# Pieces of x, loads further ahead and later weight parts in a retention and two-MLP kernel

## The chip, the cores and the metric

The kernel runs on one core of a Trainium2 chip. The metric is the device time of one execution in microseconds (us); the time before is the median of three runs. A traced execution gives the profile.

## The reference, cut to what matters

A retention layer (a linear attention with a decay per head) over 4 sequences of 768 tokens, 8 heads of 64, and behind it two MLPs over the 3072 tokens, with 512 features and 2048 hidden units:

```python
for t in range(S):
    state = gamma * state + einsum('bhd,bhe->bhde', k[:, :, t], v[:, :, t])
    y[:, :, t] = scale * einsum('bhd,bhde->bhe', q[:, :, t], state)
x = y.transpose(0, 2, 1, 3).reshape(3072, 512)
h = x @ w_in;  x = (h * cos(h)) @ w_out                    # first MLP
h = x @ w_in2                                              # second MLP
g = where(h >= 1, h, where(h <= -1, 0, (h + 1) ** 2 / 4))
out = g @ w_out2
```

All inputs are float32. The kernel's products are made of high and low parts: a matrix is split into a rounded part and the rest, and three of the four products of parts are summed.

## The kernel before, in words

Tokens run in six blocks of 512 (b = 0 to 5); hidden units in 16 slices of 128, in two halves of eight (k = 0, 1). One step is one slice of one block: `first` multiplies x by a slice of w_in (12 matmuls of 512 columns into one PSUM bank, line 642), `act` makes h cos h of it, and `second` (12 matmuls, line 729) multiplies the result by a slice of w_out into four banks that gather over eight steps. `second` runs three steps behind `first`. There are 48 steps for k = 0 and 48 for k = 1. In the first 40, attention is done in between, chunk by chunk of 128 tokens, and `first` alternates between two banks (line 1457 on); in the other 56 it uses four. The kernel is written in the order of execution for each engine; nothing is rescheduled. The second MLP, from about 640 us on, is a fast matrix product of seven half-size products (class `Products`); only its first group is touched by the change.

In `act` ScalarE rounds h to whole turns (`rounded`, line 680), VectorE takes the fraction (line 685), ScalarE the sine (line 691); a step later VectorE multiplies (line 694), ScalarE makes the high part gh (line 698) and VectorE the low part gl (line 705), which is the last to read the bank of h. The results of a block are read out by `evacuate` (lines 740 to 747): four tiles of 512 columns, made by VectorE and ScalarE, and stored by SP. For k = 1 the stored result of k = 0 is added. The tiles come from a ring of five buffers named r, which `rounded` uses too.

Data that move meanwhile: x, made by attention or needed again for k = 1, is stored by ScalarE's queue (`store_parts`, high and low part, 1 MB each) and loaded by SP (`load_parts`); partial results by `load_part`. Attention's operands for a chunk (q and k as qk and kq, v, the keys kd, the state's increments vw) are loaded by SP, as many steps ahead as the table `lead` says. Weights come as 64-bit floats of 512 KB per slice (raw) and are converted by a conveyor (`Convert`, `Conveyor`): `load`, and some steps later `one` (VectorE), `two` (ScalarE, line 192), `three` (VectorE), `four` (GpSimd, line 209), `five`. For the second MLP, `five` calls `combine`: GpSimd makes four sums of quarters of two slices (line 246), `seven` and `eight` then split them and the quarters into high parts (ScalarE, line 139) and low parts (GpSimd, line 142), and SP stores these (`send_parts`). The numbers in the conveyor's table are the steps between the load and each of these. Ready weights are weights that were converted earlier and stored; they are only loaded.

The right sides of the fast product, differences of quarters of the first MLP's output, are made by `right_sides(0)` in 22 small items, one a step: GpSimd's subtractions (line 825) and again high and low parts.

Each engine works its instructions off in order, and SP and ScalarE also issue DMAs. A program waits for a DMA at one of eight counters that SP and ScalarE share in turn, and the issue of a DMA first waits until the DMA that used the same counter before has landed, which is the one eight places before it in the program's order.

Of the kernel before, what the change touches and what calls it, by code (L numbers as in the profile page):

```python
# [40 lines left out]
def tile_retention_mlp_mlp(  # L41
# [113 lines left out]

    class Convert:
# [4 lines left out]
        def __init__(self, m, j, a, keep, late=False, ready=False, store=False):  # L161
            self.m, self.j, self.a, self.keep, self.late, self.ready = m, j, a, keep, late, ready
            self.store = store or not late

        def load(self, stage):
            self.stage = stage
            if self.ready:
                self.f = self.stage.tile([P, TB], F32, tag="cf", name="cf", bufs=5)
                nc.sync.dma_start(out=self.f, in_=w32_d[self.m, self.j, self.a])
                return  # L170
            self.raw = self.stage.tile([P, TB, 2], I32, tag="raw", name="raw", bufs=3 - self.late)
            src = (w1, w2)[self.m][self.j][:, self.a * TB:(self.a + 1) * TB]
            nc.sync.dma_start(out=self.raw.rearrange("p n w -> p (n w)"), in_=src.bitcast(I32))

        def one(self):
            if self.ready:
                return
            ncs, ncf = ((3, 3), (1, 5))[self.late]
            self.s = self.stage.tile([P, TB], I32, tag="cs", name="cs", bufs=ncs)
            self.f = self.stage.tile([P, TB], F32, tag="cf", name="cf", bufs=ncf)  # L180
# [44 lines left out]
        def combine(self):  # L225
# [55 lines left out]
    class Conveyor:  # L281
# [40 lines left out]
    class Attention:  # L322
# [41 lines left out]
        def load_t(self, n):  # L364
# [4 lines left out]
            if n >= NEW:  # L369
# [6 lines left out]
                self.kq[n] = self.ring("kq", 3 * TB // 2, 2)  # L376
                nc.sync.dma_start(out=self.kq[n], in_=kq[n - NEW])
# [6 lines left out]
        def load_v(self, n):  # L384
# [14 lines left out]
            for r in range(2):  # L399
# [214 lines left out]

    def store_parts(b):
        for t, d in zip(xt[0, b], xT_d[b]):
            nc.scalar.dma_start(out=d, in_=t.bitcast(F32))

    def load_parts(b):

        x_tiles(1, b)
        for t, d in zip(xt[1, b], xT_d[b]):
            nc.sync.dma_start(out=t.bitcast(F32), in_=d)

    def load_part(b):

        for t, d in zip(xt[1, b], (yp_d[b], yq_d)[:1 + (b == 0)]):
            t = t.bitcast(F32)
            nc.sync.dma_start(out=t, in_=d)
            for e in range(NP):  # L630
# [119 lines left out]
    class Products:  # L750
# [76 lines left out]
        def make(self, c):  # L827
# [14 lines left out]
            def parts(q):  # L842
# [9 lines left out]
                lambda: self.sums(x, ("t2", "22", "t1"), ("t4", "21", "t2")),  # L852
            ] + [lambda q=q: parts(q) for q in TURN]
# [363 lines left out]
        def run(self, before):  # L1217
# [13 lines left out]
            for g in range(self.NG + 1):  # L1231
                if g == 0:
                    ends = iter([f for b in before for f in (b, lambda: None)])
# [11 lines left out]
                if g == 0:  # L1245
# [4 lines left out]
                    top.append(self.ps)  # L1250
                    self.pairs += [("wo", n) for n in range(NH + NP + 1, NF - 1)]
# [7 lines left out]
    def run():  # L1259
        i = 0  # L1260
        with ExitStack() as es:
# [155 lines left out]
            plan = {n: [[] for _ in range(6)] for n in range(NH * (NB - 1))}  # L1417
            for n in range(CB, NCH):
                c = n % CB
                if n < 3 * CB:  # L1420
                    i = 11 * (n // CB - 1) + c
                    lead = (3, 1, 0) if n < 2 * CB else (3, 3, 1)
                else:
                    i = NH * (n // CB - 1) + 2 * c
                    lead = (4, 2, 1)
                plan[i][3 if n >= 3 * CB else 4].append(n)
                plan[i + 1][5].append(n)
                for k in range(3):
                    if n >= CB + (CB, 1, 1)[k]:
# [3 lines left out]
            for i in range(NH * (NB - 1)):  # L1433
                load_t, load_v, decay, early, late, attend = plan[i]
# [3 lines left out]
                for n in load_t:  # L1438
                    att.load_t(n)
                for n in load_v:  # L1440
# [44 lines left out]
                if i in (6, 9):  # L1485
                    store_parts(i // 9)
# [9 lines left out]
        with ExitStack() as es:  # L1496
# [5 lines left out]
            while i < len(steps):  # L1502
# [34 lines left out]
            assert not todo and not ready and not any(conv.slots[-4:])  # L1537
# [94 lines left out]
```

## Time and profile before

| | before |
|---|---|
| runs | 1117.85, 1118.36, 1120.42 us |
| median | 1118.36 us |
| profiled execution | 1123.43 us, of which span 1121.6 us |
| TensorE, matmuls | 1079.9 us busy (96% of the span) |
| VectorE, GpSimd, ScalarE | 802.5, 613.8, 602.1 us busy |
| DMA | 279.9 MB, mean 250 GB/s |
| mean granted clock | 0.987 |

Busy matmuls overlap each other, so the share of TensorE says that it seldom stands, not that it is at its peak. The granted clock is 1 at 2.4 GHz and 0.5 at 1.2 GHz, the two levels in this trace. Where TensorE stands, the trace names the engine and line that released it.

### The profile page before, as it was taken

The page shows a single profiled execution, that of the slowest core. Times are in us where ns is not written, and L with a number is a line of the kernel's source. Part 1 is how long each engine was busy: PE and PEld are TensorE (multiplying, and loading weights), DVE is VectorE, ACT ScalarE, POOL GpSimd, SP SyncE. Part 2 cuts the span into 40 slices and gives each one's busy share as a digit, 9 for nine tenths or more (in the row PEclk, how much of TensorE's full clock was granted, in tenths as well). Part 3 has the DMA queues.
Part 4 walks back from the last instruction along what each step waited for, and adds up shares of the span by engine and source line. Part 5 has one row for each costly group of instructions (what it writes and reads, how often), then busy time and mean ns, then how long its engine had stood idle before and what let it go on. Part 6 is the DMA issues. An engine that isn't in the chain of part 4 may idle for free.

```text
span 1121.6 us, 17830 instructions
## 1 busy us (share of the span) xinstructions
PE 1079.9 (96%) x6286; PEld 873.4 (78%) x6286; DVE 802.5 (72%) x1101; ACT 602.1 (54%) x1078; POOL 613.8 (55%) x525
## 2 busy tenths in 40 slices
PE   7997999989999999999899999999999999999996
PEld 5676777868888888887688878787888788888884
DVE  5776867766766635677786377677888778977776
ACT  3453333323444644555555376676757677666663
POOL 3834202221225655789998057696648786464642
PEclk9999999989999999999999999999999999999999
DMA  9559488785749778878797666979779889576542
GB/s 326 176 197 318 119 236 283 223 290 179 251 137 329 254 257 288 287 290 303 240 342 250 241 219 217 316 237 361 254 221 317 305 293 387 172 243 207 182 150 85
DMA packets 126504, 279.94 MB, mean 250 GB/s; under 512 B 14032, under 2 KB 40272, under 8 KB 122448
## 3 DMA queue, kind: packets, MB, share of 16 engines
q1 hardware_dynamic: 119792, 257.31, 69.0%
q10 hardware_dynamic: 6624, 21.50, 4.9%
q8 instruction: 50, 0.82, 0.3%
q14 instruction: 38, 0.31, 0.1%
HBM read 195.39 MB, written 83.36 MB: 249 GB/s over the span
## 4 chain that ended last, share of the span: by engine, by line
PE 79%; DVE 6%; DMA 5%; POOL 5%; issue 3%; ACT 2%; SPq 1%; DVEq 0%; ACTq 0%; POOLq 0%
PE b L729 20%; PE b L642 20%; PE b L911 17%; PE y L927 17%; PE b L557 1%; PE b L464 1%; DMA qk<-in_qk 1%; POOL s L246 1%; DVE big L993 1%; DMA xb1t20h<-xhi 1%; POOL cf L209 1%; POOL cf L142 1%; DVE cf L185 1%; DMA xb2t20h<-xhi 1%; PE b L475 1%
## 5 line engine op out<-in xcount | busy, mean ns | idle before, releaser
L685 DVE SCALAR_TENSOR_TENSOR r<-b,r 128x512 f32<-128x512 f32 x96 | 66.1, 689 | 141.0 <-ACT r L680 140.4
L209 POOL TENSOR_TENSOR cf<-cf,cs 128x512 int32<-128x512 int32 x64 | 83.2, 1300 | 144.3 <-DVE cf L200 115.3
L680 ACT ACTIVATE r<-b 128x512 int32<-128x512 f32 x96 | 56.9, 593 | 193.3 <-PE b L642 157.3
L985 DVE TENSOR_TENSOR xh<-y,xh 128x1024 f32<-128x1024 f32 x88 | 107.1, 1221 | 27.9 <-PE y L927 26.8
L1063 POOL TENSOR_TENSOR ft<-r,f 128x512 f32<-128x512 f32 x24 | 31.1, 1296 | 139.9 <-PE y L927 93.0
L729 PE MATMUL b<-gh,wo 128*128 128x512 f32 x384 | 100.2, 396 | 5.2 <-DVE o L740 5.2
L927 PE MATMUL y<-wi,wo 128*128 128x512 f32 x360 | 92.7, 392 | 3.9 <-POOL wi L952 2.2
L642 PE MATMUL b<-xh,wi 128*128 128x512 f32 x384 | 94.9, 389 | 0.0
L729 PEld LDWEIGHTS b<-gh,wo 128*128 128x128 f32 x384 | 72.4, 191 | 22.5 <-ACT wih L139 4.6
L911 PE MATMUL b<-wih,wi 128*128 128x512 f32 x320 | 88.0, 393 | 0.4 <-DVE b L1055 0.4
L985 DVE TENSOR_TENSOR xl<-y,xl 128x1024 f32<-128x1024 f32 x64 | 77.9, 1217 | 13.8 <-PE y L927 13.8
L927 PE MATMUL y<-gh,wo 128*128 128x512 f32 x272 | 85.4, 396 | 2.3 <-DVE xh L985 2.3
L642 PE MATMUL b<-xh,wih 128*128 128x512 f32 x192 | 77.6, 407 | 7.7 <-DVE gl L705 6.1
L642 PEld LDWEIGHTS b<-xh,wi 128*128 128x128 f32 x384 | 72.1, 188 | 15.0
L927 PEld LDWEIGHTS y<-wi,wo 128*128 128x128 f32 x360 | 66.9, 188 | 20.8 <-POOL wi L952 3.7
L729 PE MATMUL b<-gh,woh 128*128 128x512 f32 x192 | 78.1, 412 | 0.5 <-ACT woh L139 0.5
L642 PE MATMUL b<-xh,wil 128*128 128x512 f32 x192 | 76.3, 400 | 0.0
L698 ACT ACTIVATE gh<-b 128x512 fp32r<-128x512 f32 x96 | 57.1, 595 | 35.0 <-DVE b L694 35.0
L729 PE MATMUL b<-gh,wol 128*128 128x512 f32 x192 | 74.5, 393 | 0.0
L952 POOL TENSOR_TENSOR gl<-ft,gh 128x512 fp32r<-128x512 f32 x56 | 71.7, 1298 | 1.3 <-ACT gh L139 1.3
L911 PEld LDWEIGHTS b<-wih,wi 128*128 128x128 f32 x320 | 60.3, 189 | 13.8 <-DVE b L1055 1.3
L691 ACT ACTIVATE r<-r 128x512 f32<-128x512 f32 x96 | 60.5, 631 | 15.2 <-DVE r L685 15.1
(164 smaller groups left out, 2752.9 us busy)
## 6 DMA issues: line engine op xcount, KB each, us to landing
wi<-wp SPq DMA_DIRECT2D x66, 512.0 KB, 4.9
wo<-wp SPq DMA_DIRECT2D x66, 512.0 KB, 5.1
raw<-in_w SPq DMA_DIRECT2D x64, 512.0 KB, 5.5
wp<-whi SPq DMA_DIRECT2D x48, 256.0 KB, 2.5
wp<-s SPq DMA_DIRECT2D x32, 256.0 KB, 2.2
w<-cf ACTq DMA_DIRECT2D x26, 256.0 KB, 3.8
xTh<-xh ACTq DMA_DIRECT2D x6, 1024.0 KB, 6.7
xTl<-xl ACTq DMA_DIRECT2D x6, 1024.0 KB, 8.8
```

Of the source, the lines that this page charges most:

```text
L209: nc.gpsimd.tensor_tensor(out=f, in0=f, in1=self.s, op=ALU.add)
L642: nc.tensor.matmul(out=h, lhsT=w[:, c * P:(c + 1) * P], rhs=x[:, c, :], start=(i == 0), stop=(i == len(terms) - 1),)
L680: nc.scalar.activation(out=self.r.bitcast(I32), in_=self.h, func=AF.Identity, scale=INV_2PI, bias=0.25)
L685: nc.vector.scalar_tensor_tensor(out=self.r, in0=self.h, scalar=INV_2PI, in1=self.r.bitcast(I32), op0=ALU.mult, op1=ALU.subtract,)
L691: nc.scalar.activation(out=self.r, in_=self.r, func=AF.Sin, scale=TWO_PI, bias=HALF_PI)
L698: nc.scalar.activation(out=self.gh, in_=self.h, func=AF.Copy)
L729: nc.tensor.matmul(out=acc[k, b][e], lhsT=w[:, s], rhs=g, start=(begin and i == 0), stop=(last and i == 2),)
L911: nc.tensor.matmul(out=to, lhsT=w[:, c * P:(c + 1) * P], rhs=x, start=begin and n == 0, stop=n == len(terms) - 1, skip_group_check=not begin,)
L927: nc.tensor.matmul(out=to[:, e, :], lhsT=w[:, e * P:(e + 1) * P], rhs=a, start=begin and m == 0, stop=m == 2, skip_group_check=not begin,)
L952: eng.tensor_tensor(out=lo, in0=self.f.pop((g, q)), in1=hi.bitcast(F32), op=ALU.subtract)
L985: nc.vector.tensor_tensor(out=a, in0=y, in1=a, op=ALU.add)
L1063: nc.gpsimd.tensor_tensor(out=o, in0=x, in1=z, op=ALU.subtract)
```

## The change

x moves in pieces: `store_parts` and `load_parts` only list pieces of one of four feature groups (256 KB); `send_x` issues two of them on ScalarE behind each step, `fetch_x` three on SP. Blocks 0 and 1 are listed after steps 3 and 6, where their stores stood at steps 6 and 9. Partial results come in two halves. Attention's loads get a table with four columns (q, k and state together; kq; v and keys; decay). In the stage of the second MLP's weights the conveyor has one step more before `one` and two more before `seven` and `eight`, one more raw buffer, and keeps its parts in weight buffers that are free by then (`spare_tile`) in place of two-buffer rings. `right_sides(0)` starts at the first step of the fifth block for k = 1 (before: the fifth step of the third), one item a step in that block and two in the last. The last second products stand one place later in the first group of the fast product, and its accumulators' tiles are named once before use.

```diff
+    spare = (
+        {
+            "f": [f"il{n}" for n in range(NH)] + [f"ol{n}" for n in range(6)],
+            "s": [f"ih{n}" for n in range(NH)],
+            "whi": [f"oh{n}" for n in range(NH)] + ["ol6", "ol7"],
+        },
+        {
+            "f": ("il1", "il3", "il5", "il7", "ol1", "ol3"),
+            "s": ("ih3", "ih5", "ih7", "ih1"),
+            "whi": ("oh1", "oh3", "oh5", "oh6", "oh7", "ol5", "ol6", "ol7"),
+        },
+    )
+    spare = [{nm: itertools.cycle(tags) for nm, tags in d.items()} for d in spare]
+
+    def spare_tile(nm, few, dt=F32):
+        return wpool[0].tile([P, TB], dt, tag="w" + next(spare[few][nm]), name=nm)
...
+            self.few = (j // 2 * 4 + a * 2 + j % 2) > 18
...
-            self.raw = self.stage.tile([P, TB, 2], I32, tag="raw", name="raw", bufs=3 - self.late)
+            self.raw = self.stage.tile([P, TB, 2], I32, tag="raw", name="raw", bufs=3 + self.late)
...
-                t = wpool[0].tile([P, TB], F32, tag=f"wo{'hl'[n]}6", name=f"s{n}")
+                t = spare_tile("s", self.few)
...
-            if n in (1, 2):
-                hi = self.stage.tile([P, TB], F32R, tag="whi", name="whi", bufs=2)
-            else:
-                hi = wpool[0].tile([P, TB], F32R, tag=f"wo{'hl'[n // 3]}7", name="whi")
+            hi = spare_tile("whi", self.few, F32R)
...
-                order = (("five", 2), ("one", 1), ("two", 1), ("three", 1), ("four", 1), ("seven", 3), ("eight", 3))
+                order = (("five", 3), ("one", 2), ("two", 2), ("three", 2), ("four", 2), ("seven", 5), ("eight", 5))
...
+    pieces = []
+
     def store_parts(b):
-        for t, d in zip(xt[0, b], xT_d[b]):
-            nc.scalar.dma_start(out=d, in_=t.bitcast(F32))
+        for c in range(NP):
+            for t, d in zip(xt[0, b], xT_d[b]):
+                pieces.append((d[:, c, :], t[:, c, :].bitcast(F32)))
+
+    def send_x():
+        for d, t in pieces[:2]:
+            nc.scalar.dma_start(out=d, in_=t)
+        del pieces[:2]
...
+    def fetch_x():
+        for t, d in coming[:3]:
+            nc.sync.dma_start(out=t, in_=d)
+        del coming[:3]
...
-                    ends = iter([f for b in before for f in (b, lambda: None)])
+                    none = lambda: None
+                    ends = iter([before[0], none, none, before[1], none, before[2]])
...
-                    lead = (3, 1, 0) if n < 2 * CB else (3, 3, 1)
+                    lead = (3, 0, 1, 0)
+                    if n >= NEW:
+                        lead = (6, 5 if c < 2 else 1, 6 if c < 3 else 2, 1)
                 else:
                     i = NH * (n // CB - 1) + 2 * c
-                    lead = (4, 2, 1)
+                    lead = (3, 2, 2, 1)
...
-                if i in (6, 9):
-                    store_parts(i // 9)
+                send_x()
+                if i in (3, 6):
+                    store_parts(i // 6)
                 elif i >= 2 * NH and i % NH == 2:
                     store_parts(steps[i][1])
...
-                conv.start(todo.pop(0) if todo and (l < 7 if k == 0 else l % 4 != 3) else None, stage)
+                now = l < NH - 1 if k == 0 else l != NH - 1 and (l != 3 or b > 2) or len(todo) > len(order2) - READY
+                conv.start(todo.pop(0) if todo and now else None, stage)
                 first(k, b, j, 4 + i % 4)
+                fetch_x()
                 send_parts()
                 done = second(i - LAG)
                 n = blocks.index((k, b)) + 1
                 if k == 1 and l == NH - 1:
-                    load_part(b)
+                    load_part(b, range(2))
+                elif k == 1 and l == 0 and b:
+                    load_part(b - 1, range(2, NP))
...
-                if (k, b, l) == (1, 2, LAG + 1):
+                if (k, b, l) == (1, 4, 0):
                     ready = fast.right_sides(0)
-                if ready:
+                for f in ready[:1 if b < NB - 1 or l == 1 else 2]:
                     fill.append(ready.pop(0))
                 act(k, b, j, done, fill)
+                send_x()
```

ScalarE, before, around the store of block 3's x (xTh and xTl are its high and low part, w a converted weight, cs a conversion, r the rounding, gh a high part, o a result of block 2):

```order
L218 DMA w_0_12_0_90<-cf 128x512
L192 ACTIVATE cs<-raw 128x512
L617 DMA xTh_63<-xh 128x2048
L617 DMA xTl_64<-xl 128x2048
L680 ACTIVATE r<-b_2665 128x512
L698 ACTIVATE gh<-b_2556 128x512
L139 ACTIVATE xh<-b_2679 128x4x128
L691 ACTIVATE r<-r 128x512
L218 DMA w_0_12_1_91<-cf 128x512
L192 ACTIVATE cs<-raw 128x512
L680 ACTIVATE r<-b_2732 128x512
L698 ACTIVATE gh<-b_2665 128x512
L691 ACTIVATE r<-r 128x512
```

After, the same place:

```order
L239 DMA w_0_12_1_91<-cf 128x512
L213 ACTIVATE cs<-raw 128x512
L647 DMA xTh_63<-xh 128x512
L647 DMA xTl_64<-xl 128x512
L719 ACTIVATE r<-b_2750 128x512
L737 ACTIVATE gh<-b_2676 128x512
L730 ACTIVATE r<-r 128x512
L239 DMA w_0_13_0_92<-cf 128x512
L213 ACTIVATE cs<-raw 128x512
L647 DMA xTh_63<-xh 128x512
L647 DMA xTl_64<-xl 128x512
L719 ACTIVATE r<-b_2842 128x512
```

The two whole stores become two pieces behind each of four steps, each pair ahead of a rounding r; the first pair stands where a step more is done.

SP, before, at the store of block 2's results (yp; qk and kq are of one chunk, v, w for the state and kd of the chunk before it):

```order
L173 DMA raw<-in_w 128x1024 x2
L373 DMA qk<-in_qk 64x512 x2
L377 DMA kq<-in_kq 128x768
L398 DMA v<-in_v 128x512
L401 DMA w_2151<-in_vw 64x512 x2
L419 DMA kd<-in_kn 128x512
L747 DMA yp_77<-o 128x512 x4
L173 DMA raw<-in_w 128x1024
L373 DMA qk<-in_qk 64x512 x2
```

After, the same place:

```order
L189 DMA raw<-in_w 128x1024
L391 DMA qk<-in_qk 64x512 x2
L424 DMA w_2158<-in_vw 64x512 x2
L189 DMA raw<-in_w 128x1024
L419 DMA kq<-in_kq 128x768
L414 DMA v<-in_v 128x512
L442 DMA kd<-in_kn 128x512
L786 DMA yp_77<-o 128x512 x4
L189 DMA raw<-in_w 128x1024
L391 DMA qk<-in_qk 64x512 x2
```

kq leaves its place behind qk and comes a step later, with v and kd; w for the state comes with qk.

GpSimd, before, in the stage of the second MLP's weights (cf are converted weights, s0 and s1 the sums, whi ScalarE's high parts, cs a conversion; wih, wil, woh and wol belong to the right sides):

```order
L825 TENSOR_TENSOR wih3_5638<-wol1_5645,woh3_5639 128x512
L825 TENSOR_TENSOR wih1_5641<-wil5_5644,wih3_5638 128x512
L246 TENSOR_TENSOR s0_5765<-cf_5657,cf_5701 128x256
L246 TENSOR_TENSOR s1_5766<-cf_5657 128x256
L246 TENSOR_TENSOR s0_5765<-s0_5765,cf_5657 128x256
L246 TENSOR_TENSOR s1_5766<-cf_5701,s0_5765 128x256
L142 TENSOR_TENSOR wil7_5808<-wih3_5638,wih7_5807 128x512
L209 TENSOR_TENSOR cf_5812<-cf_5812,cs_5811 128x512
L142 TENSOR_TENSOR s0_5765<-s0_5765,whi_5818 128x512
L142 TENSOR_TENSOR s1_5766<-s1_5766,whi_5821 128x512
L142 TENSOR_TENSOR cf_5701<-cf_5701,whi_5824 128x256
L142 TENSOR_TENSOR cf_5657<-cf_5657,whi_5827 128x256
```

After, a place in the same stage (f are the converted weights, s both sums):

```order
L267 TENSOR_TENSOR s_4972<-f_4930 128x256
L267 TENSOR_TENSOR s_4973<-f_4885,f_4930 128x256
L267 TENSOR_TENSOR s_4972<-s_4972,f_4885 128x256
L267 TENSOR_TENSOR s_4973<-f_4885,s_4972 128x256
L142 TENSOR_TENSOR s_4878<-s_4878,whi_4978 128x512
L142 TENSOR_TENSOR s_4879<-s_4879,whi_4981 128x512
L142 TENSOR_TENSOR f_4816<-f_4816,whi_4984 128x256
L142 TENSOR_TENSOR f_4712<-f_4712,whi_4987 128x256
L142 TENSOR_TENSOR f_4816<-f_4816,whi_4987 128x256
L230 TENSOR_TENSOR f_5050<-f_5050,cs_5049 128x512
L230 TENSOR_TENSOR f_5100<-f_5100,cs_5099 128x512
L142 TENSOR_TENSOR s_4972<-s_4972,whi_5106 128x512
```

Before, the sums s0_5765 are split in the step after the one that made them. After, the sums s_4972 are split behind the parts of the pair before them and two more additions (rows with f and cs), a step later, and no right sides stand between.

## Rows read from the trace of the kernel before

**Rows 1.** Waits of TensorE: line waited for: us in total, times, longest

```profile
PE b L642 <- DVE gl L705: 6.1, 2, 4.0
...
PE b L729 <- DVE o L740: 5.2, 2, 4.2
```

**Rows 2.** Stretches: length, busy us of PE, PEld, DVE, ACT, POOL; clock, DMA, GB/s

```profile
80.00:100.00 20.00, 20.00 (x90) 16.54 (x90) 15.83 (x24) 10.51 (x19) 10.03 (x8) 1.00 1.01 323
100.00:120.00 20.00, 13.76 (x196) 10.93 (x195) 12.11 (x21) 5.10 (x9) 7.41 (x6) 0.83 0.70 188
```

**Rows 3.** Timeline of TensorE: start us, us, instruction [idle before, releaser]

```profile
111.79 1.98 PE L557 MATMUL b<-qk,w 128*64 128x64 f32 x32 [6.24 <-issue]
...
115.57 0.60 PE L729 MATMUL b<-gh,woh 128*128 128x512 f32 x1
...
116.00 0.40 PE L729 MATMUL b<-gh,wol 128*128 128x512 f32 x1
...
173.92 0.71 PE L642 MATMUL b<-xh,wih 128*128 128x512 f32 x1 [2.05 <-DVE gl L705]
...
177.41 1.10 PE L642 MATMUL b<-xl,wih 128*128 128x512 f32 x4
...
233.86 0.80 PE L642 MATMUL b<-xh,wih 128*128 128x512 f32 x1 [4.04 <-DVE gl L705]
...
237.44 1.75 PE L642 MATMUL b<-xl,wih 128*128 128x512 f32 x4
...
559.95 3.56 PE L729 MATMUL b<-gh,wo 128*128 128x512 f32 x8 [4.25 <-DVE o L740]
...
647.81 1.20 PE L911 MATMUL b<-woh,wi 128*128 128x512 f32 x4 [1.34 <-DVE b L1055]
```

**Rows 4.** Timeline of all engines, 88 to 108 us

```profile
89.37 0.33 ACTq L617 DMA_DIRECT2D xTh<-xh  x1
...
97.74 1.11 SPq L401 DMA_DIRECT2D w<-in_vw  x2
...
99.59 0.65 SPq L173 DMA_DIRECT2D raw<-in_w  x1
...
107.06 0.45 DVE L182 TENSOR_SCALAR cf<-raw 128x512 f32<-128x512 f32 x1 [6.31 <-DMA raw<-in_w]
```

**Rows 5.** DMA issues, 80 to 100 us: count, KB each, median us to landing

```profile
raw<-in_w SPq DMA_DIRECT2D x3, 512.0 KB, 6.3
...
xTh<-xh ACTq DMA_DIRECT2D x1, 1024.0 KB, 8.4
```

**Rows 6.** DMA issues, 58 to 80 us

```profile
raw<-in_w SPq DMA_DIRECT2D x3, 512.0 KB, 3.8
```

**Rows 7.** Timeline of all engines, 225 to 240 us

```profile
225.68 4.13 SPq L747 DMA_DIRECT2D yp<-o  x4
...
228.96 0.33 ACTq L617 DMA_DIRECT2D xTh<-xh  x1
...
231.88 0.60 ACT L680 ACTIVATE r<-b 128x512 int32<-128x512 f32 x1 [5.69 <-DMA yp<-o]
```

**Rows 8.** Timeline of all engines, 549 to 560 us

```profile
552.88 1.43 POOL L246 TENSOR_TENSOR s<-cf 128x256 f32<-128x256 f32 x2
...
555.04 0.63 ACT L139 ACTIVATE whi<-s 128x512 fp32r<-128x512 f32 x1 [2.27 <-POOL s L246]
...
557.91 0.69 DVE L685 SCALAR_TENSOR_TENSOR r<-b,r 128x512 f32<-128x512 f32 x1 [6.90 <-ACT r L680]
```

**Rows 9.** DMA issues, the whole execution (the page's part 6)

```profile
w<-cf ACTq DMA_DIRECT2D x26, 256.0 KB, 3.8
```

**Rows 10.** Timeline of ScalarE, 66 to 78 us

```profile
71.63 0.60 ACT L680 ACTIVATE r<-b 128x512 int32<-128x512 f32 x1 [2.77 <-PE b L642]
...
77.07 0.60 ACT L680 ACTIVATE r<-b 128x512 int32<-128x512 f32 x1 [2.76 <-PE b L642]
```

**Rows 11.** A stretch of 45 us, columns as in rows 2

```profile
545.00:590.00 45.00, 40.76 (x174) 33.30 (x173) 34.13 (x44) 23.31 (x44) 42.13 (x39) 0.96 0.81 286
```

More of the change, by code (lines that the diff above doesn't have):

```diff
@@ L167, in load @@
             if self.ready:
-                self.f = self.stage.tile([P, TB], F32, tag="cf", name="cf", bufs=5)
-                nc.sync.dma_start(out=self.f, in_=w32_d[self.m, self.j, self.a])
                 return
-            self.raw = self.stage.tile([P, TB, 2], I32, tag="raw", name="raw", bufs=3 - self.late)
+            self.raw = self.stage.tile([P, TB, 2], I32, tag="raw", name="raw", bufs=3 + self.late)
             src = (w1, w2)[self.m][self.j][:, self.a * TB:(self.a + 1) * TB]
@@ L176, in one @@
             if self.ready:
+                self.f = spare_tile("f", self.few)
+                nc.sync.dma_start(out=self.f, in_=w32_d[self.m, self.j, self.a])
                 return
-            ncs, ncf = ((3, 3), (1, 5))[self.late]
-            self.s = self.stage.tile([P, TB], I32, tag="cs", name="cs", bufs=ncs)
-            self.f = self.stage.tile([P, TB], F32, tag="cf", name="cf", bufs=ncf)
+            n = 3 - self.late
+            self.s = self.stage.tile([P, TB], I32, tag="cs", name="cs", bufs=n)
+            if self.store:
+                self.f = self.stage.tile([P, TB], F32, tag="cf", name="cf", bufs=n)
+            else:
+                self.f = spare_tile("f", self.few)
             f = self.f.bitcast(I32)
@@ L375, in load_t @@
                     )
-                self.kq[n] = self.ring("kq", 3 * TB // 2, 2)
-                nc.sync.dma_start(out=self.kq[n], in_=kq[n - NEW])
                 return
@@ L398, in load_v, with load_kq, load_w @@
             nc.sync.dma_start(out=t[h], in_=v[n][h])
-            for r in range(2):
+        def load_kq(self, n):
+            if n >= NEW:
+                self.kq[n] = self.ring("kq", 3 * TB // 2, 2)
+                nc.sync.dma_start(out=self.kq[n], in_=kq[n - NEW])
+        def load_w(self, n):
+            for r in range(2 if n >= NEW else 0):
                 h = slice((1 - r) * D, (2 - r) * D)
@@ L852, in make @@
                 lambda: self.sums(x, ("t2", "22", "t1"), ("t4", "21", "t2")),
+                lambda: None,
             ] + [lambda q=q: parts(q) for q in TURN]
@@ L1250, in run @@
                     top.append(self.ps)
+                    for i in range(2):
+                        self.ps.tile([P, 2, TB], F32, tag=f"y{i}", name=f"y{i}")
                     self.pairs += [("wo", n) for n in range(NH + NP + 1, NF - 1)]
@@ L1413, in opening @@
                     y[1].six()
-            plan = {n: [[] for _ in range(6)] for n in range(NH * (NB - 1))}
+            plan = {n: [[] for _ in range(7)] for n in range(NH * (NB - 1))}
             for n in range(CB, NCH):
@@ L1421, in run @@
                     i = 11 * (n // CB - 1) + c
-                    lead = (3, 1, 0) if n < 2 * CB else (3, 3, 1)
+                    lead = (3, 0, 1, 0)
+                    if n >= NEW:
+                        lead = (6, 5 if c < 2 else 1, 6 if c < 3 else 2, 1)
                 else:
                     i = NH * (n // CB - 1) + 2 * c
-                    lead = (4, 2, 1)
[L1426 to L1429, printed above, removed]
+                    lead = (3, 2, 2, 1)
+                plan[i][4 if n >= 3 * CB else 5].append(n)
+                plan[i + 1][6].append(n)
+                for k in range(4):
+                    if n >= CB + (CB, 1, 1, 1)[k]:
                         plan[i - lead[k]][k].append(n)
@@ L1433, in run @@
             for i in range(NH * (NB - 1)):
-                load_t, load_v, decay, early, late, attend = plan[i]
+                load_t, load_kq, load_v, decay, early, late, attend = plan[i]
                 now = 5 <= i < 12 if i < 2 * NH else (i < 3 * NH + 4 or i % 2 or i > 33) and bool(todo)
@@ L1439, in run @@
                     att.load_t(n)
+                    att.load_w(n)
+                for n in load_kq:
+                    att.load_kq(n)
                 for n in load_v:
@@ L1536, in run @@
             send_parts()
-            assert not todo and not ready and not any(conv.slots[-4:])
+            assert not todo and not ready and not any(conv.slots[-6:])
+        load_part(NB - 1, range(2, NP))
         fast.run([lambda i=i: evacuate(iter(second(i)), NP) for i in range(i - LAG, i)])
```

12 lines of the change are left out of this document (7 added, 5 removed).

## The prediction

> **What bounds the kernel now.** I read the waits of TensorE first. It is busy in nearly every slice of the page, so only its holes can be won, and of the long ones three lines name the cause: the first product waits for a VectorE subtraction (6.1 us in two holes), the second product for an evacuation (5.2 us in two) [rows 1]. Then the 20 us stretches: in 100 to 120 us TensorE works 13.8 of 20 us at a granted clock of 0.83, just behind a stretch in which the DMA engines were busy all the time [rows 2]. The timeline of TensorE gives each hole and what the clock costs behind it: a matmul of 512 columns that takes 0.6 us at the lower level (1.2 GHz instead of 2.4) is back at 0.4 us at 116.00, and the long rows at 177.41 and 237.44 mark the same for the next two; eight that need 7 x 0.23 + 0.4 = 2.0 us (24 in a step of 5.44 us) take 3.56 [rows 3, 10]. Half of a stretch at the lower level is lost. So the holes cost:
>
> A, at 112 us: 6.2 hole and (116.0 - 111.8)/2 = 2.1, 8.3 us.
> B, at 174 us: 2.05 and 3.5/2 = 1.7, 3.8 us.
> C, at 234 us: 4.0 and 3.6/2 + (1.75 - 1.10) = 2.4, 6.4 us.
> D, at 560 us: 4.25 and 1.6, with a hole of 1.0 before it (5.2 in two, rows 1), 6.8 us.
> E, at 648 us: 1.3 us [rows 3].
>
> Together 26.6 us. Each has its chain, read backwards in the timeline of all engines. A: a 1 MB store of x goes out at 89.4 and needs 8.4 us; SP's loads of the state go out at 97.7 only, because each issue waits for the landing of the DMA eight places before it in the program, and that one is the store; so the raw weights are asked for at 99.6 only, and VectorE, which works in order, stands 6.3 us at their conversion until 107.1, with the masks of the next attention chunk behind it [rows 4, 5]. C (and B alike): the four evacuated results go out from 225.7 on, one by one until 229.8, beside a 1 MB store; they share five buffers with the rounding of the next step, and ScalarE's rounding stands 5.7 us until one has landed [rows 7]. In this stage the first product has two banks, so the one after next needs that step's subtraction. D: ScalarE's high parts of weight sums wait 2.3 us for GpSimd, which made the sums in the same 5 us, the rounding comes after them, and VectorE stands 6.9 us; the evacuation is behind it [rows 8]. E's hole names an addition of VectorE behind the last evacuations [rows 3].
>
> **The change, part by part.** The sum is made against the profiled execution, 1123.43 us (span 1121.6). It lies 5.1 us above the median of the three runs, 1118.36; I take it that the holes were smaller there. As nearly all of them leave the sum, what is left holds for both, and I subtract nothing for it.
>
> *x in pieces.* Twelve stores of 1 MB become 48 of 256 KB, two behind a step's work on ScalarE (the rows of its order); the loads back become three a step, the loads of partial results two and two. No byte goes away. What goes is a 1 MB transfer in the chain of eight (8.4 us) and beside the evacuated results; a 256 KB store on the same queue takes 3.8 us [rows 5, 9]. For A, B and C the sum takes out 18.5 us. The bounds for what stays are 0 and all of it; I take 2 us for A and 1 each for B and C. A keeps most because its loads now come together: in steps 5 to 8 raw weights, five parts of a chunk and two pieces are 2.4 MB in 5.44 us (the distance of two roundings, rows 10), 0.44 MB/us, where a full stretch carried 0.32 [rows 2]. Four such steps leave about 2.5 MB, 8 us, behind. The raw weights asked for in step 8 are converted some 10.9 us later and need 3.8 unhindered [rows 6], so they come a little late.
>
> *Operands of attention.* The second and third groups of chunks ask for q, k and the state five or six steps ahead, for v and the keys likewise where buffers are free; from then on q, k and state come three steps ahead, kq two. Before, kq stood in front of its fellows on SP and waited for a scores matmul of the same step, so v, state and keys came in a burst with the evacuated results behind them (the rows of SP's order); now SP is free when these come. This is part of A to C and has no price of its own. Nothing waits newly on SP but the later kq, whose buffer was freed two steps before.
>
> *Weights a step later.* One more step lies between the load and the conversion, and two steps instead of one between GpSimd's sums and ScalarE's high parts (the rows of GpSimd's order). ScalarE's 2.3 us in D go. The first right sides move from the third to the fifth block of this stage, away from most conversions. I take D out but for 1 us. What is late next is GpSimd: the fifth block gets 48 of its instructions (6 additions, 16 sums, 18 low parts, 8 of the right sides); at 42.1 us for 39 [rows 11] these are 52 us in a block of 8 times 5.44 = 43.5. It ends 8 us behind, which is less than the two steps, 10.9 us, that its readers leave; so nothing in the sum, and up to 6 us in the range, because the stores of weights wait for it on SP in front of half the partial results.
>
> *The other tiles* (parts of weights in freed weight buffers instead of two) cost no instruction. *The last second products* one place later, and the accumulators' tiles named early: E's evacuations have one more product's time, 0.5 us stay.
>
> Sum: 1123.4 - 26.6 + (2 + 1 + 1 + 1 + 0.5) = 1102.3 us.
>
> **Rivals.** *The traffic only moves.* A, B and C come back elsewhere, because the bytes are the same and the steps 5 to 8 ask for more than the engines carry. For it: 323 GB/s at a full share in 80 to 100 us, and raw weights at 6.3 us there against 3.8 before [rows 2, 5, 6]. Against it: the holes came from single long transfers that others waited for, not from the mean. D and E alone go, and a third of A to C: 1123.4 - 8.1 - 18.5/3 + 1.5 = 1111 us. The Trainium skill, "DMA: Bandwidth & Descriptors", section "Issuing engines are not separate DMA queues", would have it so: transfers of all issuing engines run on the same 16 DMA engines and interleave, and another queue saves issuing time only. The trace agrees as far as the slower raw loads go; it does not say that a wait behind one long transfer stays.
>
> *ScalarE waits at its own issues (slower).* It works in order, and the next rounding stands behind two issues that each wait for the DMA eight places before, now about one step. ScalarE has 2.8 us to spare there [rows 10]; so a neighbour that lands later than 5.44 + 2.8 = 8.2 us after it was asked for makes TensorE late, as the 5.7 us in C did. There are 20 such steps while the first product has two banks. At 2 us each in 15 of them: 1096.8 + 30 = 1127 us; it decides from 11 steps on (1118.4). Against it: the longest of these rows, 8.4 us, belongs to a 1 MB transfer in the fullest stretch, and the piece has 3.8.
>
> *It doesn't do what it says:* the holes have other causes, and new ones of the same size stand at the same places: 1118 us.
>
> **How the numbers follow.** Forecast 0.62, its own range 1095 (nothing of A to E left, and up to 2 us off holes behind 650 us that the change doesn't touch) to 1107; traffic only moves 0.23 (1106 to 1117); no effect 0.05; slower 0.10. The range for 8 in 10 takes in the first and nearly all of the second: 1095 to 1116. A difference of 0.2%, 2.2 us, is about what a measurement of this kernel can tell from no change. Faster by more: 0.62 + 0.22; within: 0.05; slower: 0.11.
>
> **What would show it.** Right: no hole over 2 us on TensorE before 600 us, the granted clock at 1.00 in the stretches of A to D, no ScalarE rounding that waits for a landing, raw weights not waited for by VectorE for over 2 us. Wrong: ScalarE idle before roundings with a DMA named in the steps with pieces (the slower rival), a new hole between 60 and 130 us behind VectorE's conversions (traffic), or GpSimd full from 545 to 590 with a hole of TensorE at 595 to 610 (the right sides).

## The result, and the profile after

| | before | after |
|---|---|---|
| median | 1118.11 us (1117.75 to 1120.42, 4 runs) | 1104.66 us (1102.34 to 1108.42, 4 runs) |
| ratio | | 0.9879, 95% interval 0.9848 to 0.9909 |
| profiled execution, span | 1123.43, 1121.6 us | 1102.34, 1100.5 us |
| TensorE's matmuls, busy | 1079.9 us | 1071.2 us |
| mean granted clock | 0.987 | 0.996 |

The change wins 13.5 us by the medians and 21.1 us by the two profiled executions: that of before is slower than each of its four timed runs, that of after is the fastest of its four. The waits of TensorE after (line waited for: us in total, times, longest) answer to [rows 1]:

```profile
PE b L580 <- issue: 2.6, 2, 1.5
PE b L951 <- ACT wih L139: 2.4, 1, 2.4
...
PE b L768 <- DVE o L779: 1.7, 1, 1.7
...
PE b L681 <- DVE gl L744: 0.6, 1, 0.6
```

The first product waits 0.6 us for VectorE's subtraction where it waited 6.1, the second 1.7 us for an evacuation where it waited 5.2. New at the top stands the fast product (L951), which waits for a right side. Two stretches answer to [rows 2], and two more show the end of the first MLP (columns as in rows 2):

```profile
80.00:100.00 20.00, 19.37 (x86) 15.68 (x85) 14.59 (x22) 9.68 (x18) 10.30 (x9) 1.00 0.94 317
100.00:120.00 20.00, 17.43 (x246) 13.59 (x244) 18.21 (x30) 7.61 (x14) 8.32 (x7) 1.00 0.43 142
580.00:600.00 20.00, 18.32 (x80) 14.65 (x79) 7.44 (x12) 3.85 (x7) 9.12 (x9) 1.00 0.91 290
600.00:620.00 20.00, 16.93 (x72) 13.06 (x72) 7.36 (x11) 10.53 (x20) 11.84 (x10) 1.00 0.60 222
```

From 100 to 120 us TensorE works 17.4 us instead of 13.8, at a clock of 1.00 instead of 0.83; what it lacks now lies at 600. Its timeline has these holes (start us, us, instruction, idle before and releaser), against [rows 3]:

```profile
106.41 1.15 PE L580 MATMUL b<-qk,w 128*64 128x64 f32 x32 [1.10 <-issue]
...
116.06 1.15 PE L580 MATMUL b<-qk,w 128*64 128x64 f32 x32 [1.47 <-issue]
```
```profile
584.32 1.36 PE L768 MATMUL b<-gh,wo 128*128 128x512 f32 x4 [1.68 <-DVE o L779]
...
605.95 2.11 PE L768 MATMUL b<-gh,wo 128*128 128x512 f32 x8 [0.29 <-ACT gh L737]
...
611.79 0.73 PE L951 MATMUL b<-wih,wi 128*128 128x512 f32 x2 [2.38 <-ACT wih L139]
...
613.15 0.50 PE L951 MATMUL b<-wil,wi 128*128 128x512 f32 x1 [0.40 <-POOL wil L142]
```

A is 1.1 and 1.5 us, B and C are gone, D and E too. Two new ones, called F and G from here on, stand at the end: F at 584 us (1.7 us) and G at 606 to 613 us (0.3 + 2.4 + 0.4 us). The timeline of all engines round A, against [rows 4], and at the place of C, against [rows 7]:

```profile
89.94 8.83 SPq L189 DMA_DIRECT2D raw<-in_w  x3
...
96.16 1.15 DVE L203 TENSOR_SCALAR cf<-raw 128x512 f32<-128x512 f32 x1 [1.09 <-DMA raw<-in_w]
...
101.96 0.33 SPq L419 DMA_DIRECT2D kq<-in_kq  x1
```
```profile
210.61 4.68 SPq L786 DMA_DIRECT2D yp<-o  x4
...
216.51 0.60 ACT L719 ACTIVATE r<-b 128x512 int32<-128x512 f32 x1 [3.36 <-DMA yp<-o]
```

Three raw weights now go out on SP from 89.9 us on, ahead of kq at 102.0, and VectorE waits 1.1 us for one, not 6.3. At the place of C ScalarE's rounding still waits 3.4 us for a stored result; TensorE doesn't notice. In the stage of the second weights four more roundings wait for stored results (yT), before 0.4 us in all:

```profile
ACT r L719 <- DMA yT<-o: 17.7, 4, 5.9
```

TensorE doesn't notice these either.

How much each stretch takes is read from the starts of ScalarE's roundings, one a step, which are equal where nothing disturbs (the 18 steps from the 41st take 97.92 us in all runs but e4). In us, with the runs of the next section:

| run | ratio to before | to 5th | 12th to 18th (A) | 18th to 23rd (B) | 23rd to 34th (C) | 59th to the end of the fast product |
|---|---|---|---|---|---|---|
| before | 1 | 57.1 | 54.5 | 38.7 | 80.9 | 679.8 |
| after | 0.9879 | 55.9 | 48.6 | 33.9 | 74.4 | 676.2 |
| e1 pieces | 0.9984 | 58.9 | 55.3 | 35.1 | 79.1 | 677.8 |
| e2 leads | 0.9964 | 56.5 | 48.4 | 33.7 | 78.1 | 679.0 |
| e3 both | 0.9894 | 57.4 | 48.9 | 34.0 | 74.9 | 678.0 |
| e4 late part | 1.0028 | 58.5 | 56.2 | 34.0 | 80.5 | 679.3 |
| e5 sides early | 0.9949 | 58.4 | 48.6 | 34.4 | 73.8 | 686.0 |
| e6 order on SP | 0.9890 | 55.4 | 48.6 | 34.2 | 73.9 | 677.3 |
| e7 old distances | 0.9842 | 58.5 | 48.4 | 34.3 | 74.1 | 672.5 |
| e8 after again | 0.9891 | 58.7 | 48.4 | 34.5 | 73.9 | 678.3 |
| e9 e7 and e6 | 0.9809 | 57.7 | 48.9 | 33.7 | 74.3 | 669.7 |
| e10 sides only | 0.9965 | 58.1 | 48.6 | 33.8 | 74.2 | 686.8 |
| e11 middle distances | 0.9831 | 57.7 | 48.6 | 34.9 | 73.7 | 673.3 |
| e12 sides, ends | 0.9946 | 58.4 | 48.6 | 34.1 | 76.3 | 685.1 |

(The last column ends at the hole in which the fast product's last matmuls wait 0.6 us for ScalarE.) Of the 21.1 us, A gave 5.9, B 4.7, C 6.5, the late part 3.6, the start 1.2; 1.0 went back between the 5th and the 12th step. B's 4.7 do not come in every execution: e4, whose program is that of before up to the 40th step, takes 34.0 us there, with A and C as before.

### The profile page after: what moved, and what is told of

It reads as the page before. It is cut to its first block, busy times and chain, and to the rows that moved or that the text cites. A ratio compares the mean times of both kernels' runs of the same rounds, so it can differ in the third digit from the quotient of the medians.

```text
span 1100.5 us, 17904 instructions
## 1 busy us (share of the span) xinstructions
PE 1071.2 (97%) x6286; PEld 867.0 (79%) x6286; DVE 802.5 (73%) x1101; ACT 603.3 (55%) x1078; POOL 614.9 (56%) x525
## 4 chain that ended last, share of the span: by engine, by line
PE 78%; DMA 9%; DVE 5%; ACT 2%; POOL 2%; issue 2%; SPq 1%; ACTq 0%; DVEq 0%; POOLq 0%
PE b L768 20%; PE b L681 20%; PE b L951 17%; PE y L967 16%; PE b L580 2%; DMA wo<-wp 1%; DMA xTl<-xl 1%; PE b L487 1%; DVE big L1033 1%; DMA qk<-in_qk 1%; DMA xb2t20h<-xhi 1%; DMA xb1t20h<-xhi 1%; PE b L498 1%; DMA wp<-whi 1%; DMA xh<-xTh 1%
## 5 line engine op out<-in xcount | busy, mean ns | idle before, releaser
L719 ACT ACTIVATE r<-b 128x512 int32<-128x512 f32 x96 | 57.1, 595 | 193.1 <-PE b L681 149.9
L230 POOL TENSOR_TENSOR cf<-cf,cs 128x512 int32<-128x512 int32 x42 | 54.3, 1293 | 145.0 <-DVE cf L221 109.7
L951 PE MATMUL b<-wih,wi 128*128 128x512 f32 x320 | 87.4, 390 | 2.8 <-ACT wih L139 2.4
L737 ACT ACTIVATE gh<-b 128x512 fp32r<-128x512 f32 x96 | 57.1, 594 | 39.3 <-DVE b L733 39.0
L681 PE MATMUL b<-xh,wil 128*128 128x512 f32 x192 | 74.4, 390 | 0.0
L951 PEld LDWEIGHTS b<-wih,wi 128*128 128x128 f32 x320 | 59.8, 188 | 16.4 <-ACT wih L139 2.8
L733 DVE TENSOR_TENSOR b<-b,r 128x512 f32<-128x512 f32 x96 | 66.6, 694 | 2.5 <-ACT r L730 0.3
```

The costliest lines, as they stand in the source:

```text
L230: nc.gpsimd.tensor_tensor(out=f, in0=f, in1=self.s, op=ALU.add)
L681: nc.tensor.matmul(out=h, lhsT=w[:, c * P:(c + 1) * P], rhs=x[:, c, :], start=(i == 0), stop=(i == len(terms) - 1),)
L719: nc.scalar.activation(out=self.r.bitcast(I32), in_=self.h, func=AF.Identity, scale=INV_2PI, bias=0.25)
L733: nc.vector.tensor_tensor(out=self.h, in0=self.h, in1=self.r, op=ALU.mult)
L737: nc.scalar.activation(out=self.gh, in_=self.h, func=AF.Copy)
L951: nc.tensor.matmul(out=to, lhsT=w[:, c * P:(c + 1) * P], rhs=x, start=begin and n == 0, stop=n == len(terms) - 1, skip_group_check=not begin,)
```

## Experiments

**Pieces and leads apart (e1 to e3) and the late part alone (e4).** Run together, against 1118.98 us of before.

```diff
 e1, on the kernel before: x in pieces; e3 has them too
+    pieces = []
+    def send_x(): ...
+    def fetch_x(): ...
+    load_part(b, range(2)) ... load_part(b - 1, range(2, NP))
 e2, on the kernel before: the table of leads; e3 has it too
-                    lead = (3, 1, 0) if n < 2 * CB else (3, 3, 1)
+                    lead = (3, 0, 1, 0)
+                    if n >= NEW:
+                        lead = (6, 5 if c < 2 else 1, 6 if c < 3 else 2, 1)
 e4, on the changed kernel: all of e3 taken back
```

e1. 

> The kernel before with x in pieces alone (stores, loads, partial results in halves); attention's leads, the conveyor, the right sides and the last second products as before. Theory 1 (one long store in front of those who wait makes holes A, B and C): 18.5 us of holes fall to about 4, D and E stay: 1103 to 1106 us, and the holes at 112, 174 and 234 us are under 2 us each. Theory 2 (the order on SP, kq ahead of its fellows, makes them): the pieces alone give a third, about 1112 us, and B or C stays over 2 us. Theory 3 (the bytes only move): 1112 us or more with new holes before 130 us.

e2. 

> The kernel before with attention's leads alone (q, k and state together, kq on its own); x still goes in transfers of 1 MB. Theory 1 (long store): 1115 to 1119 us, A stays over 4 us, B and C lose at most half. Theory 2 (order on SP): B and C go, 10 us, and part of A: 1104 to 1109 us.

e3. 

> The kernel before with pieces and leads, nothing else of the change. Theory 1: no better than the pieces alone by more than 2 us. Theory 2: as the leads alone, 1104 to 1109. If each holds a part of the cause, both together give 16 us in the first 240 us, as the changed kernel's trace shows there, and D (6.8 us) and E (1.3 us) stay: about 1102 to 1106 us, both single ones clearly above.

e4. 

> The changed kernel without pieces and without the new leads: only the later conveyor, its tiles, the right sides in the last two blocks and the last second products. By the two traces D gives 5.9 us, E 1.3 us, and the new holes at 584 and 606 to 613 us take 4.8 us: 1114 to 1118 us. If instead the stage of the second weights carries the gain: 1106 to 1110 us. A, B and C stand as before, 8, 4 and 6 us with the clock.

Measured: 1117.10, 1115.11, 1107.81 and 1121.73 us; intervals of the ratio 0.9965 to 1.0003, 0.9941 to 0.9988, 0.9869 to 0.9919, 1.0002 to 1.0054. Theory 1 falls: the pieces alone win 1.9 us by the medians, which the interval does not tell from nothing, and A stays. The timeline of e1 there:

```profile
97.79 4.04 SPq L401 DMA_DIRECT2D w<-in_vw  x2
...
102.57 0.36 SPq L173 DMA_DIRECT2D raw<-in_w  x1
...
109.40 0.47 DVE L182 TENSOR_SCALAR cf<-raw 128x512 f32<-128x512 f32 x1 [5.91 <-DMA raw<-in_w]
...
114.15 1.12 PE L557 MATMUL b<-qk,w 128*64 128x64 f32 x16 [6.10 <-issue]
```

SP still stands between the two loads of the state, and the next raw weight goes out at 102.6. SP's waits from 80 to 110 us show for what, first before, then in e1 (line waited for: us in total, times, longest):

```profile
SPq L401 <- DMA xTh<-xh: 4.7, 1, 4.7
```
```profile
SPq L401 <- DMA xTl<-xl: 3.1, 1, 3.1
SPq L401 <- DMA raw<-in_w: 2.0, 2, 1.6
```

It is a store of x in both: a piece of 256 KB holds SP for 3.1 us where the whole store held it for 4.7. All of SP's waits for landings in this stretch, added up from the same two answers, are 12 us in each. The pieces are not as short as the prediction took them to be, and nor are the converted weights from which it took their time, 3.8 us [rows 9]. In the changed kernel (DMA issues: count, KB each, median us to landing):

```profile
w<-cf ACTq DMA_DIRECT2D x26, 256.0 KB, 5.4
xTh<-xh ACTq DMA_DIRECT2D x24, 256.0 KB, 5.7
xTl<-xl ACTq DMA_DIRECT2D x24, 256.0 KB, 6.2
```

In e1 the operands of a whole step stand between two raw weights, and the issue of each waits for whatever DMA was eight places before. kq's waits for the scores' matmul, 53.9 us in all before, have no part in A, and at C (223 us) kq waits 0.3 us.

C stays in e1 too, without any whole store: the rounding waits for the first stored result, which goes out behind the same operands at 224.9.

```profile
230.51 0.60 ACT L696 ACTIVATE r<-b 128x512 int32<-128x512 f32 x1 [4.46 <-DMA yp<-o]
```

That result lands 5.5 us after its issue in e1 and 5.8 us before, so the 1 MB stores beside it cost little there. But before, ScalarE also stood at the issues of these two stores, 2.7 us until v and 2.2 us until that same result had landed, with the rounding of [rows 7] right behind the second:

```profile
231.46 0.33 ACTq L617 DMA_DIRECT2D xTl<-xl  x1
```

The leads take the operands away from between the raw weights and end A with the whole stores kept: 48.4 us in e2. But alone they move the stall: before the 12th step e2 loses 5.3 us (a rounding waits 5.6 us for stored results beside the whole stores), and C stays, by way of ScalarE's own issue:

```profile
230.60 0.33 ACTq L218 DMA_DIRECT2D w<-cf  x1
230.97 0.66 ACT L192 ACTIVATE cs<-raw 128x512 int32<-128x512 uint32 x1 [6.46 <-DMA qk<-in_qk]
...
233.49 0.50 PE L647 MATMUL b<-xh,wih 128*128 128x512 f32 x1 [3.30 <-DVE gl L710]
```

The conversion cs stands 6.5 us behind the issue of a converted weight, which waits for the landing of a qk. Only both together end C (74.9 us). So each part is worth 2 to 4 us alone, by the medians, and 11.2 together. No theory holds as it stands: e1 is above the times of the first two, e2 has theory 1's time without theory 1's A, and e3 is 2 us above its range. e4 tells that the late part, by itself, costs 3 us (0.2 to 6 by the interval): D and E go, but holes of 1.7 and 2.1 us come at 380 and 469 us, and in the place of G stands a hole of 4.9 us, with 0.5 and 0.4 behind it and half the clock from 625 to 631 us. On top of the early part the late part wins 3.1 us by the medians (e3 against after), and the intervals overlap.

**What made F and G, and what ended D (e5 to e8).** Against 1119.57 us.

```diff
 e5: first half of the right sides four steps earlier, second half as it was
-                if (k, b, l) == (1, 4, 0):
-                    ready = fast.right_sides(0)
+                if (k, b, l) == (1, 3, 4):
+                    ready = fast.make(0)
+                if (k, b, l) == (1, 5, 2):
+                    ready += fast.make(1)
-                for f in ready[:1 if b < NB - 1 or l == 1 else 2]:
+                for f in ready[:1 if b < NB - 1 else 2]:
 e6: fetch_x, load_part, then send_parts (after: fetch_x, send_parts, load_part)
 e7: the conveyor's old distances, as five 3 -> 2, one 2 -> 1, seven 5 -> 3
 e8: the changed kernel, unchanged
```

e5. 

> The changed kernel with the first half of the right sides four steps earlier (from the fifth step of the fourth block; the second half stays in the last block). Theory 1 (GpSimd's lateness makes the holes at 584 and at 606 to 613 us, because stores of weights wait for its low parts on SP and the loads behind them): both holes fall below 1 us, 4 us less than the changed kernel, 1100 to 1102 us. Theory 2 (the holes come from the traffic of the last block): unchanged, 1104 to 1106 us, holes of 1.7 and 2.4 us as before.

e6. 

> The changed kernel with one order turned on SP: a step's loads of partial results stand ahead of its stores of weights. GpSimd stays as late as it was. Theory 1: the hole at 584 us goes (1.7 us), the one at 606 to 613 us stays, since the loads of the right sides' second half and the results still stand behind the stores: 1102 to 1104 us. Theory 2 (partial results asked for too late in themselves): both stay.

e7. 

> The changed kernel with the conveyor's old distances (two steps to GpSimd's low parts, one between load and conversion, three to the second split); tiles and right sides as changed. Theory 1 (ScalarE's high parts wait for GpSimd's sums, D): a hole of TensorE of 3 to 5 us behind the evacuation comes back in the fourth or fifth block, 1108 to 1112 us. Theory 2 (moving the right sides away is what ended D): no such hole, 1103 to 1106 us.

e8. 

> The changed kernel once more, unchanged, as the measure for the three beside it: 1102 to 1108 us, with the holes at 584 us and at 606 to 613 us between 1 and 3 us each if they belong to the program's order, and absent if they were an accident of the one profiled execution.

Measured: 1112.09, 1104.56, 1099.09 and 1104.77 us; intervals 0.9921 to 0.9978, 0.9851 to 0.9930, 0.9809 to 0.9874, 0.9856 to 0.9926. e8 has F at 587 us (1.9 us) and G at 616 us (2.4 and 0.4): they belong to the program. In the changed kernel's timeline of all engines one sees how they come:

```profile
579.59 1.06 SPq L669 DMA_DIRECT2D xh<-yp  x2
...
582.33 2.51 POOL L142 TENSOR_TENSOR s<-s,whi 128x512 fp32r<-128x512 f32 x2
583.57 1.32 DVE L779 TENSOR_TENSOR o<-b,xh 128x512 f32<-128x512 f32 x2 [2.03 <-DMA xh<-yp]
...
584.87 0.32 SPq L296 DMA_DIRECT2D wp<-s  x1
...
588.30 2.02 SPq L786 DMA_DIRECT2D yT<-o  x4
...
590.41 0.59 SPq L860 DMA_DIRECT2D wil<-yT  x1
```
```profile
597.57 1.29 POOL L864 TENSOR_TENSOR woh<-wih,wil 128x512 f32<-128x512 f32 x1 [10.64 <-DMA wih<-yT]
...
601.67 0.63 ACT L139 ACTIVATE wih<-wih 128x512 fp32r<-128x512 f32 x1 [8.95 <-POOL wih L864]
```

The second half of the partial results (xh<-yp, L669) is asked for at 579.6, behind eight stores of weights, and the evacuation waits 2.0 us for it: F. GpSimd's low parts of the last weights run until 587; their stores (wp) hold SP until 588, and only then come the results' stores and the loads of the right sides' second half (yT). GpSimd starts on these at 597.6, ScalarE's first high part is made at 601.7, and the fast product waits for the last ones: G. e6 turns the order on SP: F goes, as theory 1 said. G's chain stays, one place earlier: at 605 TensorE waits 3.0 us for a high part gh that ScalarE makes behind the same right sides, and the clock is at half from 605 to 611 us. The time is that of e8; the 1.7 us that theory 1 expected are less than the intervals can tell. With the old distances (e7) the last store of weights goes out at 582 us (in e8 at 590), G goes and 5.7 us are won, though theory 1 expected a loss; no run of e7 (1097.59 to 1100.60) is as long as any of e8 (1102.40 to 1107.78). ScalarE's waits in e7, then before (380 to 620 us):

```profile
ACT whi L139 <- POOL s L267: 12.3, 12, 3.5
```
```profile
ACT whi L139 <- POOL s L246: 7.4, 6, 3.3
```

The wait on which the prediction put D is longer in e7 than before, 12.3 us in twelve against 7.4 in six; after, the same answer has no such line. And D's chain does come back in e7, earlier and smaller:

```profile
447.94 0.63 ACT L139 ACTIVATE whi<-s 128x512 fp32r<-128x512 f32 x1 [3.50 <-POOL s L267]
...
450.74 0.69 DVE L724 SCALAR_TENSOR_TENSOR r<-b,r 128x512 f32<-128x512 f32 x1 [3.51 <-ACT r L719]
...
452.77 2.43 PE L768 MATMUL b<-gh,wo 128*128 128x512 f32 x8 [1.68 <-DVE o L779]
```

ScalarE waits for the sums, VectorE for the rounding and TensorE for the evacuation, as in [rows 8], but for 1.7 us and in the third block. Behind it, from 460 to 700 us, e7 has no hole above 0.6 us. So the longer distances take out a wait that is worth 1.7 us in e7, and cost 5.7.

e5, for which theory 1 expected a gain, is 6 us above both theories. It keeps F (1.3 us) and G (2.1 and 0.4 us), has two waits for x of 1.3 and 1.5 us (478 and 524 us) and brings a hole at D's place back without ScalarE's wait for sums. With the first half of the right sides among the conversions, a store of weights keeps a buffer that VectorE's conversion wants:

```profile
540.85 0.67 DVE L203 TENSOR_SCALAR f<-raw 128x512 f32<-128x512 f32 x1 [10.73 <-DMA wp<-f]
...
548.05 2.47 PE L768 MATMUL b<-gh,wo 128*128 128x512 f32 x5 [5.84 <-DVE o L779]
```

VectorE stands 10.7 us and TensorE 5.8. One reading fits e5, e7 and the next runs: D is too much work for GpSimd and its stores in one place, whichever engine shows it. No run changes that work alone.

**Which part of the late change (e9 to e12).** Against 1118.77 us.

```diff
 e9: e7 and e6 together
 e10: e3, and the right sides in the last two blocks as changed
 e11: distances between old and new
-    ("five", 3), ("one", 2), ... ("seven", 5), ("eight", 5)
+    ("five", 3), ("one", 2), ... ("seven", 4), ("eight", 4)
 e12: e10, and the last second products as changed
```

e9. 

> The changed kernel with the conveyor's old distances and, on SP, a step's loads of partial results ahead of its stores of weights. Theory 1 (with the stores of weights earlier, the two holes of 0.4 and 0.5 us at 584 to 586 us are what the order on SP still costs): they go, nothing new behind them: 1097 to 1099 us. Theory 2 (as in the run of the order alone, what is won at 584 is lost in the next wait): 1099 to 1101 us, with a hole between 600 and 615 us.

e10. 

> The kernel before with pieces, leads and the right sides in the last two blocks; conveyor, its tiles and the last second products as before. Theory 1 (the right sides filled GpSimd among the conversions, and that was D): the holes at 495 and 543 us of the run with pieces and leads (0.7 and 3.8 us, and 1.6 us of clock) go: 1101 to 1104 us, E's hole of 1.5 us stays. Theory 2 (the rings of two buffers made D): D stays, 1106 to 1109 us.

e11. 

> The changed kernel with distances between old and new: one step more between load and conversion, but the second split one step behind the sums as before the change, so the last parts come one step later than with the old distances and one earlier than with the new. Theory 1 (the lateness of the last parts is the price): half of 5.7 us: 1101 to 1103 us, with holes of under 1.5 us near 585 and 612 us. Theory 2 (the step between load and conversion is the price): as the changed kernel, 1104 to 1106 us. Theory 3 (the double distance of sums and split is): as with the old distances, 1098 to 1100 us.

e12. 

> As the run with the right sides beside it, and the last second products one place later with the accumulators named early. Theory 1 (E's hole is a wait for the last evacuations): 1.3 us less than that run, no hole over 0.5 us near 630 us on a wait for VectorE's additions; 1100 to 1102 us. Theory 2: the hole turns up one product later, same time. If the tiles of the conveyor are worth something beside, it stays above the changed kernel with old distances (1099).

Measured: 1096.76, 1114.30, 1100.11 and 1112.82 us; e10 0.9948 to 0.9982, e12 0.9929 to 0.9963. e9 is the fastest kernel of the study, 0.9809 (0.9778 to 0.9840) against 0.9891 (0.9856 to 0.9926) of e8; its trace has neither F nor G, and e7's two holes at 584 to 586 us are gone, as theory 1 said; the 2.3 us between e7 and e9 are inside the intervals. e11 is on the level of e7 (0.9831 and 0.9842): its G is gone, but its F is 3.7 us, which no theory said. So most of the 5 us is the price of the last split's second step behind the sums, and the step between load and conversion costs nothing that shows. How much of the 5 us is left in e11 its interval (0.9811 to 0.9851) doesn't tell, so theories 1 and 3 both stay open. e10 missed both theories: D's holes at 495 and 543 us are gone, but it is 6.5 us slower than e3:

```profile
581.40 0.63 ACT L139 ACTIVATE whi<-s 128x512 fp32r<-128x512 f32 x1 [5.36 <-POOL s L246]
...
584.17 0.69 DVE L706 SCALAR_TENSOR_TENSOR r<-b,r 128x512 f32<-128x512 f32 x1 [5.43 <-ACT r L701]
...
586.20 2.04 PE L750 MATMUL b<-gh,wo 128*128 128x512 f32 x4 [5.20 <-ACT cs L192]
```
```profile
608.62 0.74 POOL L246 TENSOR_TENSOR s<-cf,s 128x256 f32<-128x256 f32 x1
...
614.22 2.07 PE L750 MATMUL b<-gh,wo 128*128 128x512 f32 x4 [4.56 <-ACT gh L719]
```

This is D's chain of before [rows 8], 26 us later: ScalarE waits 5.4 us for GpSimd's sums, VectorE 5.4 for the rounding, and TensorE stands 5.2. The last sums are made at 608.6 us, in the middle of the right sides' second half; after, they are made at 573.4. In the changed kernel the sides can move back because the conversions are done earlier: the last raw weight is asked for at 578 us in e10, at 553 after and at 548 in e7. That can be the work of the changed rule that starts conversions (`now` in the diff), of the added buffers (four for raw where there were two, so two more and not one, and two for cs where there was one) or of the other tiles; which of them was not tried. e12 shows E alone, by its trace: e10's wait of 1.4 us for VectorE at 641 us is gone, and no hole above 0.3 us takes its place before 720 us. The two times (1.5 us apart, with overlapping intervals) cannot tell it.

## Why the prediction was right, and where its steps were not

The time was forecast at 1102, in 1095 to 1116; it is 1104.66. The sum was made against the profiled execution and came out at that of the changed kernel, 1102.3 against 1102.34 us. That is luck: the two errors cancel, and this execution is the fastest of four. For A to C the sum took out 14.5 us, and 17.1 went. For D and E it took out 6.6, and 3.6 went, because F and G came.

*A, B and C.* The holes and their costs with the clock hold, and so does what would be left. The cause holds in part. The sum took all of it out for the pieces and gave the leads no price of their own; e1 to e3 show that A is the leads' work and that C needs both. Two steps failed. One is the size of a piece: 3.8 us, where 5.7 and 6.2 were measured, so that with the store cut up, SP stood 3.1 us for a piece of it. The DMA eight places before was that store, as [rows 4] were read, but its length was not what made the chain. That was how many operands stand between two raw weights, as e2 shows with the whole stores in place. The other step is the wait of kq for a matmul, by which the prediction explained the burst: it is not in A's chain, and is 0.3 us at C.

*The execution that was summed.* The prediction took it that the holes were smaller in the other runs. B is that: 4.7 us against e4, so far as one other trace tells. Without it, and without 1.2 us at the start, 15.2 us are left of 21.1, near the 13.5 of the medians.

*D.* It went, but for the most part not for the reason given. The wait of ScalarE for the sums was ended by the longer distances, as said. Without them (e7) the same chain makes a hole of 1.7 us, not of 4 to 5, and the kernel is 5.7 us faster. That the conversions end earlier, in which e7 and e10 differ, the prediction doesn't speak of: the line that starts them is in the diff and was passed over.

*GpSimd in the fifth block.* Its lateness was seen, with its chain (stores of weights on SP in front of half the partial results), and put at nothing, up to 6 us in the range. F and G cost 1.7 + 0.3 + 2.4 + 0.4 = 4.8 us. What was missed: the two steps that its readers leave are themselves what makes the last stores late. The prediction's own sign came: GpSimd is busy 41.7 of the 45 us from 545 to 590 and 19.8 of the 20 from 560 to 580, and G's holes begin at 606.

*E* went, by the traces of e12 and after, as said (1.3 us).

*The rivals.* ScalarE waits at its own issues: it does, for 3.5 us at the longest in e1, 6.5 in e2, 4.8 in e3 and 2.0 in the changed kernel, but only e2's made a hole of TensorE above 0.5 us, and 20 such steps there never were. Before the change it did so at C. That no rounding would wait for a landing was wrong: 3.4 us for yp and 17.7 for yT remain, and cost TensorE nothing that the trace names. The traffic only moves: this held of e2, which lost before the 12th step most of what it won at A; with both parts, the same bytes fit. The rule of the Trainium skill ("DMA: Bandwidth & Descriptors", section "Issuing engines are not separate DMA queues") is not against it: total traffic is the same 279.9 MB, and the loads were moved in time, not to another queue. From 60 to 80 us the DMA engines' share is 0.99 where it was 0.51, and from 100 to 120 us 0.43 where it was 0.70.

*The lower bound*, 1095 with nothing of A to E left, is about what e9 reached, 1096.76.

## What to carry to other kernels

Where two parts of a change act on one queue, price them together: here 1.9 and 3.9 us alone make 11.2 together, and one part of the change (the longer distances) was a loss of 5 us hidden inside the gain. When an issue waits for an earlier DMA, ask how much is queued between the urgent loads, not only which DMA it waited for. A quarter of the bytes is not a quarter of the wait: a store of 1 MB landed after 8.4 us in the kernel before, one of 256 KB after 5.7 in the changed one. A longer distance in a pipeline takes waits out of its middle and makes its end later; look at who waits for the last item.

## What was not expected of the hardware

The first loads of q and k land at times that differ from one execution to the next: TensorE's longest wait for them is 1.1 us in e6 and 2.6 in e1, and the 5th rounding begins between 55.4 and 58.9 us in 14 executions whose code differs little there. Between the two traced executions of the changed kernel that is 2.8 us, against 2.4 us between their spans. A hole of 1.4 or 1.5 us in the first 10 us left the granted clock at 1.00 (before, e2), one of 1.7 us took it to 0.5 (e3), and behind one of 2.5 us it was 0.5 from 8 to 14 us (e8). It is not the length alone: G's 2.4 us at 612 and 616 us (after, e8) left it at 1.00, as F's 1.7 us did in the changed kernel, while behind F's 1.9 us in e8 it was 0.5 from 588 to 591 us.
